# A transformer block's sum kernel: two attention-times-V blocks of a chunk joined, the last one moved within W2, and the next chunk's normalisation in other units

## The chip, the core and the metric

The kernel runs on one core of one Trainium2 chip. The metric is the device time of one execution in microseconds; the lower the better. Engines are named as the profile names them: PE is TensorE (matmuls), PEld its weight loads, DVE is VectorE, ACT is ScalarE, POOL is GpSimd, SP is SyncE, which issues most DMAs. ACTq and SPq are the DMA issues on ScalarE's and SyncE's own instruction queues.

## What is computed

All tensors are bf16: x is 1 x 2048 x 576, with 32 heads of 18, a causal window of 256 keys, and a gated feed-forward layer of width 4608. Both branches read the same normalised x, and the result is their sum with x.

```python
def _A_ref(x, wqkv, wo):
    B, S, D = x.shape
    H = 32; Dh = D // H; W = 256
    qkv = ...(x @ wqkv).reshape(B, S, 3, H, Dh)...
    scores = jnp.einsum("bhqd,bhkd->bhqk", q, k) * (Dh ** -0.5)
    mask = (idx[:, None] - idx[None, :] >= 0) & (idx[:, None] - idx[None, :] < W)
    p = _softmax(jnp.where(mask[None, None], scores, -1e9), axis=-1)
    o = jnp.einsum("bhqk,bhkd->bhqd", p, v)
    return ...(o)... @ wo

def _B_ref(x, w1, w3, w2):
    return (silu(x @ w1) * (x @ w3)) @ w2

xn = _layernorm(x, axis=-1)
return x + _A_ref(xn, A_wqkv, A_wo) + _B_ref(xn, B_w1, B_w3, B_w2)
```

## The kernel before

The 2048 rows go in four chunks of 512 (chunk 0 to 3, `c`). A chunk has three stretches on PE. First the projections of q, k and v (`PROJ`, line 490). Then 36 units of gate/up (`unit_pairs`, line 726): unit `u` makes 128 of the 4608 hidden columns in nine pairs of matmuls, one matmul of a pair on the upper and one on the lower 64 rows of the array, 512 columns each. Its two banks go through ACT (`unit_tanh`, line 735) and two DVE operations (`unit_h`, lines 741 and 744) into `hT[u]`; the second of these frees the unit's banks. Last W2 and the output projection (`p2_list`, `p2_item`, line 797), a list of steps of two matmuls each, counted by `n`.

Attention is spread between the units. Eight groups of four heads (`g`) have four score steps each in chunk 0 and five in the later chunks. A score step (`score_step`) is four or six matmuls of line 610 into the fixed banks 6 and 7 (`SC`), one exponential on ACT over both (line 619), and masks on POOL (line 646). The next score step overwrites those two banks, so it waits for that exponential. The exponentials stay in slots: `pt` (10), the stage tiles (4, `sh`), and the last tiles of `hT`, as long as their units have not come (`early`). `spaced_step` sets the steps by `clock`, a count of matmul pairs.

Two groups with all their steps done make one attention-times-V block (`pv`, line 667): 72 small matmuls in chunk 0 and 96 later, eight tiles of 64 x 32 of the array at once, into a pair of banks. There are four blocks (`j`) to a chunk. Blocks 0 to 2 stand behind a unit's last pair once `PV_AFTER` = 20 counts have passed, block 3 stands in W2 at step 8. A block is drained by two DVE transposes (`pv_out`, line 676), a reciprocal and a POOL multiplication for each half (`o_scale`, lines 681 and 682), two DVE transposes a half (`o_turn`, line 689), and DMAs into `oT` (`o_pack`, line 714): four, and for block 0 eight more small ones, which chunk 0 issues on ACT's queue, one a unit.

Banks 0 to 5 are three pairs (`JOBS`) that `job()` deals out in turn to projections, units and blocks alike; whoever gets a pair waits until its last reader is done. `add` records every operation with what it reads and writes; each engine executes its operations in the recorded order, and waits are worked out from the records. `later(u, ...)` puts work behind `unit_h` of unit `u`.

The next chunk's x tiles are normalised meanwhile: `loads` (SP), `stat` (three DVE operations and two on POOL), `apply` (two on DVE) and `xt` (`xn_send`, a DMA transpose on SP into the other half of `xnT`) name the units, in `near`: 20 to 40. Weights of a group of four units come in six DMAs on SP (`load_part`), two a unit, each behind a matmul.

## Time and profile before

| what | value |
|---|---|
| time, median of 3 runs | 558.03 us (557.90 to 558.07) |
| profiled execution: span from first to last instruction | 556.1 us |
| mean granted TensorE clock | 1.000 |
| attention-times-V matmuls (line 667) | 1440 in 16 blocks |
| gate/up matmuls (line 726), 64x512 | 2592 |
| W2 and wo matmuls (line 797), 64x288 | 2524, and 45 on all rows at the end |
| oT DMAs (line 714) issued on ACT's queue | 8, of 8 KB |

The profiled execution's own time is the span; the difference to the median lies before the first and after the last instruction. A row of the timeline gives the start and the length in microseconds of one instruction or of several like ones in a row (x4), then engine, line, operation, what it writes and reads, and in brackets how long the engine had been idle and what released it. The recorded length of a matmul has the depth of the pipeline in it, so two matmuls in a row overlap; from start to start is the pace.

### The profile page before, as it was taken

What the parts mean: (1) busy time and instruction counts of PE and PEld (TensorE: products, weight loads), DVE (VectorE), ACT (ScalarE), POOL (GpSimd) and SP (SyncE); (2) the same over time, 40 slices, a digit from 0 to 9 for tenths busy, and PEclk for the clock granted to TensorE, in tenths of its full rate; (3) what the DMA queues carried; (4) which work ended last, traced back from release to release, by engine and by line L of the source; (5) the groups of instructions that cost most, each with busy time, mean ns of one, the idle gap of its engine ahead of it and who ended that gap; (6) DMA issues with size and microseconds to landing.
All of it is one profiled execution on the core that took longest, in us unless ns stands there. A gap on an engine that the chain in (4) does not pass through costs nothing.

```text
span 556.1 us, 18239 instructions
## 1 busy us (share of the span) xinstructions
PE 552.4 (99%) x8022; PEld 348.8 (63%) x8022; DVE 310.8 (56%) x587; ACT 257.6 (46%) x365; POOL 160.0 (29%) x380
## 2 busy tenths in 40 slices
PE   8999999999999999999999999999999999999998
PEld 4555445677687455477767645547777654555776
DVE  7466798610456778851056668884105567767211
ACT  7456776100286767600047776650005676666000
POOL 5323454300034445330003344533000333433000
PEclk9999999999999999999999999999999999999999
DMA  9997899677566556656856746566683684650650
GB/s 255 203 197 161 201 215 182 171 179 191 139 139 149 135 147 151 155 148 176 205 109 137 171 110 170 126 163 164 158 205 83 138 174 124 151 135 21 174 152 22
DMA packets 128038, 86.00 MB, mean 155 GB/s; under 512 B 35702, under 2 KB 125646, under 8 KB 127958
## 3 DMA queue, kind: packets, MB, share of 16 engines
q1 hardware_dynamic: 89138, 62.80, 49.7%
q10 hardware_dynamic: 38820, 22.02, 16.0%
q8 instruction: 63, 1.03, 0.8%
q14 instruction: 17, 0.14, 0.1%
HBM read 71.29 MB, written 2.36 MB: 132 GB/s over the span
## 4 chain that ended last, share of the span: by engine, by line
PE 98%; DMA 1%; ACT 0%; DVE 0%; issue 0%
PE ps L726 51%; PE ps L797 29%; PE ps L490 10%; PE ps L610 6%; PE ps L667 4%; DMA xp<-in_A_x_dram 1%; DVE stats L386 0%; ACT hT L380 0%; PE ps L419 0%; ACT sd L359 0%; ACT xnT L432 0%; DVE ofin L819 0%; DVE mv L389 0%
## 5 line engine op out<-in xcount | busy, mean ns | idle before, releaser
L726 PE MATMUL ps<-xnT,w 64*128 64x512 bf16 x1400 | 182.3, 376 | 0.0
L726 PE MATMUL ps<-xnS,w 64*128 64x512 bf16 x1120 | 155.3, 376 | 0.0
L797 PE MATMUL ps<-w,hT 64*128 64x288 bf16 x2292 | 143.9, 282 | 0.0
L741 DVE SCALAR_TENSOR_TENSOR gs<-th,ps 128x512 bf16<-128x512 bf16 x144 | 98.0, 681 | 80.1 <-ACT th L735 79.1
L619 ACT ACTIVATE pt<-ps 128x1024 bf16<-128x1024 f32 (+1 forms) x112 | 113.2, 1010 | 63.8 <-PE ps L610 62.5
L797 PEld LDWEIGHTS ps<-w,hT 64*128 64x128 bf16 x2292 | 112.0, 94 | 29.4 <-issue 0.4
L726 PEld LDWEIGHTS ps<-xnT,w 64*128 64x128 bf16 x1400 | 73.8, 94 | 55.0
L646 POOL TENSOR_TENSOR pt<-pt,mk 128x128 int32<-128x128 int32 (+1 forms) x199 | 80.3, 426 | 79.5 <-ACT pt L619 79.5
L744 DVE SCALAR_TENSOR_TENSOR hT<-gs,ps 128x512 bf16<-128x512 bf16 x144 | 98.9, 687 | 5.0
L735 ACT ACTIVATE th<-ps 128x512 bf16<-128x512 f32 x144 | 85.4, 593 | 22.2 <-PE ps L726 21.9
L726 PEld LDWEIGHTS ps<-xnS,w 64*128 64x128 bf16 x1120 | 60.1, 94 | 50.1
L503 ACT ACTIVATE stage<-ps 128x512 bf16<-128x512 f32 x16 | 9.6, 597 | 142.8 <-PE ps L490 140.5
L828 DVE TENSOR_TENSOR ofin<-ps,xp 128x288 bf16<-128x288 f32 x31 | 12.2, 451 | 110.3 <-PE ps L797 110.3
L646 POOL TENSOR_TENSOR hT<-hT,mk 128x128 int32<-128x128 int32 (+1 forms) x31 | 12.4, 420 | 170.5 <-ACT hT L619 170.5
L610 PE MATMUL ps<-qv,kv 64*128 64x320 bf16 (+4 forms) x528 | 53.8, 260 | 0.0
L610 PEld LDWEIGHTS ps<-qv,kv 64*128 64x128 bf16 x528 | 28.5, 94 | 24.7 <-issue 0.3
L490 PE MATMUL ps<-xnT,wp 64*128 64x512 bf16 (+1 forms) x360 | 39.0, 355 | 0.0
L619 ACT ACTIVATE stage<-ps 128x1024 bf16<-128x1024 f32 x24 | 24.6, 1024 | 12.6 <-PE ps L610 12.6
L689 DVE STREAM_TRANSPOSE od<-oq 128x256 bf16<-128x256 bf16 x64 | 25.8, 428 | 6.3 <-POOL oq L682 6.3
L490 PEld LDWEIGHTS ps<-xnT,wp 64*128 64x128 bf16 x360 | 20.6, 94 | 12.6 <-ACT va L539 0.4
L490 PE MATMUL ps<-wv,xnT 64*128 64x288 bf16 x288 | 22.1, 284 | 0.2 <-ACT xnT L432 0.2
L646 POOL TENSOR_TENSOR stage<-stage,mk 128x128 int32<-128x128 int32 (+1 forms) x42 | 16.9, 421 | 17.4 <-ACT stage L619 17.3
(73 smaller groups left out, 337.6 us busy)
## 6 DMA issues: line engine op xcount, KB each, us to landing
w<-in_B_w_dram SPq DMA_DIRECT2D x210, 192.0 KB, 4.3
w<-in_B_w_dram ACTq DMA_DIRECT2D x70, 288.0 KB, 3.5
xp<-in_A_x_dram SPq DMA_DIRECT2D x29, 144.0 KB, 3.3
out_dram<-ofin SPq DMA_DIRECT2D x31, 72.0 KB, 3.2
xnS<-xnT SPq DMA_DIRECT2D x8, 256.0 KB, 5.2
oT<-od SPq DMA_DIRECT2D x56, 36.0 KB
pt<-in_A_wqkv_dram SPq DMA_DIRECT2D x4, 288.0 KB, 5.0
hT<-in_B_w_dram SPq DMA_DIRECT2D x6, 192.0 KB, 6.3
```

What stands on the lines that cost most here:

```text
L490: op = add("pe", lambda e, out_=out_, st=st, mv=mv, n=n, r0=r0, first=first: e.matmul(out_, st, mv, start=first, stop=(part == 1 and n == ...
L610: add("pe", lambda e, r0=r0, out_=out_, kb=kb, q0=q0, nb=nb: e.matmul(out_, kb4[r0:r0 + 64, g, kb + NV - NB, :] if kb < 0 else kv[r0:r0 + ...
L619: add("act", lambda e: e.activation(pt_slot(sl)[:, 0:w, :], PS[:, SC[0]:SC[1] + 1, 0:w].rearrange("p r q -> p q r"), ACT.Exp, scale=scale) ...
L646: add("pool", lambda e, vb=vb, mm=mm: e.tensor_tensor(vb, vb, mm, ALU.mult), r=(key if n == 0 else []) + ["mk"], **{"w" if n == 0 else "j" ...
L667: add("pe", lambda e, p=p, q=q, pr=pr, sl=sl, g=g, pos=pos, q0=q0, nb=nb, col=col, first=first, n=n: e.matmul(PS[32 * q:32 * q + VW, banks ...
L689: add("dve", lambda e: e.transpose(od[i][:, g % 2, c0:c0 + CH // 2], oq[:, c0:c0 + CH // 2]), r=["oq", "oq0"], **{"j" if half or g % 2 els ...
L726: op = add("pe", lambda e, n=n, r0=r0, r=r, k=k, src=src: e.matmul(PS[:, b0 + r, :], wt[r0:r0 + 64, k, fl * 128:(fl + 1) * 128], src, star ...
L735: add("act", lambda e: e.activation(th[i][:], PS[:, bg, :], ACT.Tanh, scale=0.5), r=[("ps", bg)], w=[("th", i)])
L741: add("dve", lambda e: e.scalar_tensor_tensor(out=gs[i][:], in0=th[i][:], scalar=1.0, in1=PS[:, bg, :], op0=ALU.add, op1=ALU.mult), r=[("t ...
L744: add("dve", lambda e: e.scalar_tensor_tensor(out=hT[:, u, :], in0=gs[i][:], scalar=0.5, in1=PS[:, bu, :], op0=ALU.mult, op1=ALU.mult), r= ...
L797: op = add("pe", lambda e: e.matmul(PS[:, bank, 0:w], stat, move, start=new, stop=False, skip_group_check=True, **tile), r=keys, after=hel ...
L828: add("dve", lambda e: e.tensor_tensor(ofin[:, o, :], PS[:, bank, 0:HD], xp[xs[n]][:, d0:d0 + HD], ALU.add), r=[("ps", bank), ("xp", xs[n] ...
```

## The change

Blocks 0 and 1 of a chunk become one (`BLOCKS`): two bank pairs are taken at once, and the matmuls of both stand together. The joined block's place is given by unit and pair (`AT`): before pair 0 of unit 21 in chunk 0, before pairs 4, 6 and 8 of unit 18 in chunks 1, 2 and 3. Its drain is recorded right there: four transposes, four reciprocals (each half has its own `rden` now), and the first multiplication; the halves 2 and 3 are held in two `pt` slots lent for it (`borrow`). Block 2 stands at least 36 counts after its last step. Chunks 1 to 3 start with eight slots in `hT` (`NHP`, tiles 20 to 35) instead of four, and chunk 0 may use the stage tiles too. Block 3 stands at step 58 of W2 instead of 8. The next x is loaded in units 2 and 5 and normalised in units 3 to 15; in chunk 0, whose loads stay, the first two tiles in units 14 to 19 and the others as before. Of block 0's eight small packs, two are issued a unit instead of one in chunk 0, still on ACT's queue.

```diff
@@ -202,6 +202,7 @@
 
         NXP, NOF, NPT, NW13, NW2, NOD, AHEAD = 7, 4, 10, 3, 4, 2, 6
         KB, NB, NV = 64, CH // 64, 12
+        NHP = 8
         ident = sb("ident", [128, 128])
         xp = [sb(f"xp{i}", [128, D]) for i in range(NXP)]
         xn = [sb(f"xn{i}", [128, 640]) for i in range(2)]
@@ -237,22 +238,23 @@
             if kind == "sh":
                 two = stage[:, 2 * n:2 * n + 2, :]
             else:
-                two = hT[:, NF - 8 + 2 * n:NF - 6 + 2 * n, :]
+                two = hT[:, NF - 2 * NHP + 2 * n:NF - 2 * NHP + 2 + 2 * n, :]
             return two.rearrange("p t c -> p (t c)").rearrange("p (q r) -> p q r", r=2)
 
         def pt_keys(sl):
             kind, n = sl
             if kind == "pt":
-                return [("pt", n)]
+                return [(kind, n)]
             if kind == "sh":
                 return [("sh", 2 * n), ("sh", 2 * n + 1)]
-            return [("h", NF - 8 + 2 * n), ("h", NF - 7 + 2 * n)]
+            t = NF - 2 * NHP + 2 * n
+            return [("h", t), ("h", t + 1)]
 
         def st_keys(*tiles):
             return [("sh", t) for t in tiles]
 
         uq = sb("uq", [128, CH], dt.float32)
-        rden = sb("rden", [128, CH // 32], dt.float32)
+        rden = [sb(f"rden{i}", [128, CH // 32], dt.float32) for i in range(4)]
         oq = sb("oq", [128, CH])
         od = [sb(f"od{i}", [128, 2, CH]) for i in range(NOD)]
         oT = sb("oT", [128, 5, CH])
@@ -672,16 +674,26 @@
                                     r=pt_keys(sl) + [("va", pos)], **{"j" if any(k[0] == p for k in seen - {(p, gi, pr)}) or not first else "w": [("ps", banks[p])]})
                     col += nb
 
+        def borrow(slots):
+
+            for i, n in enumerate(slots):
+                uqs[2 + i:3 + i] = [pt[:, n, :, :].rearrange("p q r -> p (q r)").bitcast(dt.float32)]
+                uq_keys[2 + i:3 + i] = [[("pt", n)]]
+
         def pv_out(b, i):
-            add("dve", lambda e: e.transpose(uqs[i], PS[:, b, :]), r=[("ps", b)], w=uq_keys[i])
+            to = uqs[i]
+            add("dve", lambda e: e.transpose(to, PS[:, b, :]), r=[("ps", b)], w=uq_keys[i])
+
+        def o_recip(i):
+            u3 = uqs[i].rearrange("p (n d) -> p n d", d=32)
+            add("dve", lambda e: e.reciprocal(rden[i][:], u3[:, :, Dh]), r=uq_keys[i], w=[("rden", i)])
 
         def o_scale(i):
             u3 = uqs[i].rearrange("p (n d) -> p n d", d=32)
             o3 = oq[:, :].rearrange("p (n d) -> p n d", d=32)[:, :, 0:Dh]
-            add("dve", lambda e: e.reciprocal(rden[:], u3[:, :, Dh]), r=uq_keys[i], w=["rden"])
             add("pool", lambda e: e.tensor_tensor(
-                o3, u3[:, :, 0:Dh], rden[:].unsqueeze(2).to_broadcast([128, CH // 32, Dh]), ALU.mult),
-                r=uq_keys[i] + ["rden", "oq0"], w=["oq"])
+                o3, u3[:, :, 0:Dh], rden[i][:].unsqueeze(2).to_broadcast([128, CH // 32, Dh]), ALU.mult),
+                r=uq_keys[i] + [("rden", i), "oq0"], w=["oq"])
 
         def o_turn(g, half):
             i = g // 2 % NOD
@@ -988,7 +1000,10 @@
 
         add("act", lambda e: e.preload_act_table_set("exp_and_others"))
 
-        PV_COST, PV_AFTER = 6.6, 20
+        PV_COST, BLOCKS = 6.6, ((0, 1), (2,))
+        PV_AFTER = (18, 18, 18, 18)
+        START = (60, 46, 46, 46)
+        AT = ((21, 0), (18, 4), (18, 6), (18, 8))
         main, rest = span_main, span_last
         late_spans = {0: [(main, 2, 5, 0, 1, "act")], 1: [(main, 2, 5, 1, 2, "act"), (main, 2, 5, 2, 5, "sp")],
                       **{u: [(rest, 2, 5, u - 2, u - 1, "act")] for u in (2, 3, 4)},
@@ -998,28 +1013,30 @@
         for c in range(NC):
             NS = len(steps_of(c))
             att = [(g, s) for g in range(G) for s in range(NS)]
-            near = {0: (20, 22, 23), 1: (24, 26, 27), 2: (30, 32, 33), 3: (33, 35, 40)}
+            near = {0: (3, 5, 6), 1: (6, 8, 9), 2: (9, 11, 12), 3: (12, 14, 15)}
+            if c == 0:
+                near = {0: (14, 16, 17), 1: (16, 18, 19), 2: (30, 32, 33), 3: (33, 35, 40)}
             plan = near if c + 1 < NC else {}
             stat, apply, xt = ({v[k]: i for i, v in plan.items()} for k in range(3))
-            loads = {8: (2,), 17: (3,)} if c + 1 < NC else {}
+            loads = {2: (2,), 5: (3,)} if c + 1 < NC else {}
             if c == 0:
                 loads = {11: (0,), 13: (1,), 15: (2,), 17: (3,)}
             total = 9 * NF + len(att) + 3 * PV_COST
             if c:
                 total += 9 * sum(COST[kind] for kind, _ in PROJ)
-            start = 60 if c == 0 else 46
+            start = START[c]
             last = total - 12
             nxt = soon = start
             clock = 0.0
             done = 0
             pv_ready = {}
             free = [("pt", n) for n in range(NPT)]
-            if c:
-                free += [("sh", n) for n in range(4)]
-            early = [("h", n) for n in range(4)]
+            free += [("sh", n) for n in range(4)]
+            early = [("h", n) for n in range(4 if c == 0 else 0, NHP)]
             side = {}
             jobs = {}
             next_pv = 0
+            turned = {}
 
             def later(u, what):
                 side.setdefault(u, []).append(what)
@@ -1033,20 +1050,61 @@
                 nonlocal done
                 g, s = att[done]
                 scores(c, g, s)
-                sl = take(done)
-                exps(c, g, s, sl)
+                exps(c, g, s, take(done))
                 masks(c, g, s)
                 done += 1
-                if done % (2 * NS) == 0:
-                    pv_ready[done // (2 * NS) - 1] = clock + PV_AFTER
+                for i, pairs in enumerate(BLOCKS):
+                    if done == 2 * NS * (pairs[-1] + 1):
+                        pv_ready[i] = clock + (36 if i else PV_AFTER[c])
 
             def spaced_step():
                 nonlocal nxt, soon, clock
                 score_step()
                 soon = clock + 7.5
-                room = last - clock - PV_COST * (3 - next_pv) - 5 * sum(v > at_u for v in xt)
+                room = last - clock - PV_COST * sum(map(len, BLOCKS[next_pv:])) - 5 * sum(v > at_u for v in xt)
                 nxt = max(soon, clock + room / max(1, len(att) - done))
                 clock += 1
+
+            def pv_block(u, mid=False):
+                nonlocal next_pv, clock, free, job_ctr, nxt, soon
+                block = BLOCKS[next_pv]
+                assert u > turned.get(c, -1) + 1, (c, u, turned)
+                next_pv += 1
+                pairs = [job() for _ in block]
+                for j, banks in zip(block, pairs):
+                    pv(c, j, banks)
+                clock += PV_COST * len(block)
+                if len(block) == 2:
+                    nxt, soon = max(nxt, clock + 9), max(soon, clock + 9)
+                groups = range(2 * block[0], 2 * block[-1] + 2)
+                was = [pt_of[(c, g, s)] for g in groups for s in range(NS)]
+                assert all(NF - 2 * NHP + 2 * n > u for kind, n in was if kind == "h"), (c, u)
+                was = [sl for sl in was if sl[0] != "h"]
+                lent = [n for kind, n in was if kind == "pt"][-2:] if len(block) == 2 else []
+                free += [sl for sl in was if sl not in [("pt", n) for n in lent]] + [("pt", n) for n in lent]
+
+                def drain(pairs=pairs, lent=lent):
+                    borrow(lent)
+                    for i in range(2 * len(pairs)):
+                        pv_out(pairs[i // 2][i % 2], i)
+                    for i in range(2 * len(pairs)):
+                        o_recip(i)
+                    o_scale(0)
+
+                drain() if mid else later(u, drain)
+                job_ctr += mid
+                k = 0
+                for i, g in enumerate(groups):
+                    for half in range(2):
+                        k += 1 if (i, half) not in ((0, 1), (2, 1)) else 0
+                        later(u + k, lambda g=g, half=half: o_turn(g, half))
+                    if i + 1 < len(groups):
+                        later(u + k, lambda i=i: o_scale(i + 1))
+                turned[c] = u + k
+                for i, j in enumerate(block):
+                    later(u + 4 + 3 * i, lambda j=j: o_pack(j, "sp"))
+                    for n in range(4, 12, 2) if j == 0 else ():
+                        later(u + n // 2 + 2 + (c > 0), lambda n=n: o_pack(0, "sp" if c else "act", n, n + 2))
 
             at_u = -1
             if c:
@@ -1076,8 +1134,10 @@
                 b0 = jobs[u] = job()
                 for n in range(9):
                     into = nxt - (clock + 9 - n)
-                    if done < len(att) and (clock >= nxt or (n == 8 and into < 3 and clock >= soon)):
+                    if done < len(att) and (done < len(early) or free) and (clock >= nxt or (n == 8 and into < 3 and clock >= soon)):
                         spaced_step()
+                    if next_pv == 0 and AT[c] == (u, n):
+                        pv_block(u, True)
                     op = unit_pairs(c, u, n, n + 1, b0[0])
                     clock += 1
                     if n in (3, 8):
@@ -1085,25 +1145,8 @@
                 unit_tanh(u, b0[0])
                 if u % 4 == 3 and u < NF - 8 and (c or u != 15):
                     owed += 6
-                if next_pv in pv_ready and clock >= pv_ready[next_pv] and next_pv < 3:
-                    j = next_pv
-                    next_pv += 1
-                    banks = job()
-                    pv(c, j, banks)
-                    clock += PV_COST
-                    for g in (2 * j, 2 * j + 1):
-                        for s in range(NS):
-                            if pt_of[(c, g, s)][0] != "h":
-                                free.append(pt_of[(c, g, s)])
-                    later(u, lambda b=banks: (pv_out(b[0], 0), pv_out(b[1], 1), o_scale(0)))
-                    later(u + 1, lambda j=j: (o_turn(2 * j, 0), o_turn(2 * j, 1), o_scale(1)))
-                    later(u + 2, lambda j=j: o_turn(2 * j + 1, 0))
-                    later(u + 3, lambda j=j: o_turn(2 * j + 1, 1))
-                    later(u + 5, lambda j=j: o_pack(j, "sp"))
-                    if j == 0:
-                        for n in range(4, 12, 1 if c == 0 else 2):
-                            later(u + n + 1 if c == 0 else u + n // 2 + 4,
-                                  lambda n=n: o_pack(0, "act", n, n + 1) if c == 0 else o_pack(0, "sp", n, n + 2))
+                if next_pv in pv_ready and clock >= pv_ready[next_pv] and (next_pv or not AT[c][1]):
+                    pv_block(u)
                 unit_h(u, b0[0])
                 for what in side.pop(u, []):
                     what()
@@ -1137,7 +1180,7 @@
                     load_w2(0, (u - 20) // 2, "act" if u < 24 else "sp")
                 if u == 31:
                     xs = [load_x(c * TB + tt) for tt in range(TB)]
-            assert done == len(att) and next_pv == 3, (done, next_pv)
+            assert done == len(att) and next_pv == len(BLOCKS), (done, next_pv)
             ACC[:] = [[*JOBS[job_ctr % 3], *SC], [*jobs[NF - 2], *jobs[NF - 1]]]
             assert len({*ACC[0], *ACC[1]}) == 8
             summed.clear()
@@ -1158,18 +1201,18 @@
                             what()
                 elif n == 8:
                     load_w2(c, AHEAD - 1, after=(last_pe(),))
+                elif n == 58:
                     banks = jobs[NF - 2]
                     pv(c, 3, banks)
-                    pv_out(banks[0], 0)
-                    pv_out(banks[1], 1)
-                    o_scale(0)
-                    o_turn(6, 0)
-                    o_turn(6, 1)
-                    o_scale(1)
-                    o_turn(7, 0)
-                    o_turn(7, 1)
+                    for i in range(2):
+                        pv_out(banks[i], i)
+                        o_recip(i)
+                    for i in range(2):
+                        o_scale(i)
+                        o_turn(6 + i, 0)
+                        o_turn(6 + i, 1)
                     o_pack(3, "sp")
-                elif n == 40 and c + 1 < NC:
+                elif n == 40 and c == 0:
                     xn_send((c + 1) * TB + 3)
                 elif n == 300 and c + 1 < NC:
                     xn_swap(c + 1, ("sp", "sp"))
```

2 lines of the change are left out of this document (1 added, 1 removed).

## The prediction, as it was made before the run

> **What bounds the kernel now.** I read the page first: the busy table, then the chain that ended last.
>
> ```profile
> span 556.1 us, 18239 instructions
> PE 552.4 (99%) x8022; PEld 348.8 (63%) x8022; DVE 310.8 (56%) x587; ACT 257.6 (46%) x365; POOL 160.0 (29%) x380
> ...
> PE 98%; DMA 1%; ACT 0%; DVE 0%; issue 0%
> ```
>
> TensorE is both 99% busy and 98% of the chain, so a change moves the end only by what it adds to or takes out of TensorE's queue. The span is 556.1 us and the median 558.03, so 1.9 us lie around the span; I make the sum against 556.1 and add it unchanged to 558.03. Next I read the order of both kernels' TensorE instructions: the same matmuls, only moved. What can change is the bubbles between shapes, and new waits. So I read the timeline around an attention-times-V block (chunk 0, unit 14; columns: start, duration, engine, line, operation, tiles, shapes, count):
>
> ```profile
> 51.92 0.40 PE L726 MATMUL ps<-xnT,hT 64*128 64x512 bf16 x2
> 52.25 0.32 PE L667 MATMUL ps<-hT,va 64*20 64x320 bf16 x4
> ...
> 53.07 0.23 PE L667 MATMUL ps<-pt,va 64*20 64x128 bf16 x4
> 53.23 0.37 PE L610 MATMUL ps<-qv,kv 64*128 64x320 bf16 x4
> ...
> 53.64 0.92 ACT L619 ACTIVATE pt<-ps 128x896 bf16<-128x896 f32 x1 [0.63 <-PE ps L610]
> ```
>
> and around the end of unit 13 of the same chunk, whose score step stands after six of its nine pairs:
>
> ```profile
> 49.11 0.40 PE L610 MATMUL ps<-qv,kv 64*128 64x320 bf16 x4
> 49.33 0.61 PE L726 MATMUL ps<-xnS,hT 64*128 64x512 bf16 x4
> 49.55 1.02 ACT L619 ACTIVATE pt<-ps 128x1024 bf16<-128x1024 f32 x1 [0.54 <-PE ps L610]
> 49.76 1.26 PE L726 MATMUL ps<-xnT,hT 64*128 64x512 bf16 x10
> 50.47 0.59 ACT L735 ACTIVATE th<-ps 128x512 bf16<-128x512 f32 x1
> 50.84 0.40 PE L726 MATMUL ps<-xnS,hT 64*128 64x512 bf16 x2
> 51.09 0.69 DVE L741 SCALAR_TENSOR_TENSOR gs<-th,ps 128x512 bf16<-128x512 bf16 x1 [0.64 <-ACT th L735]
> 51.81 0.69 DVE L744 SCALAR_TENSOR_TENSOR hT<-gs,ps 128x512 bf16<-128x512 bf16 x1
> ```
>
> Five pairs take 50.84 - 49.76 = 1.08 us, so a pair takes 0.216 and streams without a gap. A score step of 512 columns takes one pair's time (49.11 to 49.33). Durations on the rows hold the pipeline's depth; starts count.
>
> **Part 1, the join: -0.8 us.** Into the block: 52.25 - 51.92 = 0.33, less the pair's 0.216, leaves 0.11. Out: 53.23 - 53.07 = 0.16, less 128 columns (a quarter pair, 0.054), leaves 0.11; the groups' starts are staggered by some 0.02, so I take 0.10 each. Joining two blocks drops one entry and one exit, 0.2 us a chunk, 0.8 in four. Bounds: 0.15 to 0.22 a chunk. The last block in W2 keeps both its bubbles.
>
> **Part 2, the wait that the join brings to chunk 0: +1.6 us.** A joined block takes two bank pairs at once. There are three pairs and the unit in progress holds one, so the second half of the block needs the pair of the unit just finished. In the built order chunk 0's block stands between the last pair of unit 20 and the first of unit 21, and the first matmul of its second half waits for VectorE's second operation (hT) of unit 20. Unit 20 has its score step after six pairs, as unit 13 above: its streaming ends at T (49.76 + 0.216 = 49.98 there), the exponential holds ScalarE until 50.57, tanh starts at 50.47, and hT ends at 51.81 + 0.69 = 52.50, T + 2.5. The first half of the block starts at T + 0.1 and takes 0.9 (52.25 to 53.23 less the exit), so the second is due at T + 1.0 and waits 1.5, and about 0.05 more for the semaphore (tanh ends at 51.06, gs starts at 51.09). TensorE is in order: units 21 and on stand behind it. Bounds: 1.3, if tanh weren't held by the exponential (chunk 1's unit 14 below, hT at T + 2.25), to 1.75, if an entry is paid again.
>
> **Part 3, the same wait in chunks 1 to 3: 0.** There the block stands inside unit 18, after 4, 6 and 8 pairs and one score step. Unit 17 of chunks 1 and 2 has its score step after three pairs, as unit 14 of chunk 1 here:
>
> ```profile
> 188.00 0.38 PE L610 MATMUL ps<-qv,kv 64*128 64x320 bf16 x6
> ...
> 189.29 0.81 PE L726 MATMUL ps<-xnT,w 64*128 64x512 bf16 x6
> 189.72 0.60 ACT L735 ACTIVATE th<-ps 128x512 bf16<-128x512 f32 x1 [0.27 <-PE ps L726]
> ...
> 191.07 0.69 DVE L744 SCALAR_TENSOR_TENSOR hT<-gs,ps 128x512 bf16<-128x512 bf16 x1
> ```
>
> It ends at 189.29 + 0.216 = 189.51; tanh starts 0.2 and hT ends 2.25 later. In chunk 1 the second half is due 4 x 0.216 + 0.216 + 0.1 + 1.2 = 2.38 after the end of unit 17 (1.2: chunk 1's half has 2560 columns to chunk 0's 1920, 0.9 x 4/3). That leaves 0.07 beyond the semaphore; chunk 2 has 0.43 more. In chunk 3 unit 17's score step follows eight pairs, hT comes some 2.9 after the end (exponential from T to T + 1.02, tanh 0.6, two operations 1.4), and the half is due at 3.24. Upper bound 0.1 a chunk. The banks go on to units 19 and 20; VectorE's four transposes (0.64 apart, rows in part 5) free the first pair before unit 19 in chunks 1 and 2, and within 0.05 us of it in chunk 3.
>
> **Part 4, two DMA issues a unit on ScalarE's queue in chunk 0: +1.2 us.** The eight small oT packs went one a unit; now two follow the tanh of each of units 25 to 28. What two issues do shows in chunk 0's unit 21, where a pack and a W2 load meet:
>
> ```profile
> 66.53 0.60 ACT L735 ACTIVATE th<-ps 128x512 bf16<-128x512 f32 x1 [0.27 <-PE ps L726]
> 66.53 0.64 ACTq L714 DMA_DIRECT2D oT<-od  x1
> 66.75 0.38 PE L610 MATMUL ps<-qv,kv 64*128 64x320 bf16 x6
> 66.97 0.59 PE L726 MATMUL ps<-xnT,w 64*128 64x512 bf16 x4
> 67.21 0.87 ACTq L352 DMA_DIRECT2D w<-in_B_w_dram  x1
> 68.13 1.02 ACT L619 ACTIVATE pt<-ps 128x1024 bf16<-128x1024 f32 x1 [1.01 <-PE ps L726]
> ...
> 68.69 0.61 ACTq L714 DMA_DIRECT2D oT<-od  x1
> ```
>
> The scores were ready at 66.97, an exponential starts 0.22 later (49.33, 49.55), but this one began at 68.13, 0.05 after the second issue ended. So issues block ScalarE. Two packs take 0.64 + 0.04 + 0.61 = 1.3 from 0.2 after a unit's end T: the next exponential starts at T + 1.55. Its successor in the order, the next score step, overwrites the same two banks and waits for it. Units 25 to 29 have their steps after 5, 4, 3, 2 pairs, then between 28 and 29 and after 7:
> - Unit 25's first issue also waits for the turn (0.43) behind unit 24's hT (T24 + 2.5), that is until T25 + 0.75. The exponential of unit 26 (0.92) then runs from T25 + 2.1 to 3.0; unit 27's step is due at T25 + 2.13 + 0.65 = 2.78: 0.3 late with the semaphore.
> - Unit 28's exponential (1.02) runs from T27 + 1.55 to 2.57; the step behind unit 28 is due at T27 + 2.16: 0.45 late.
> - The step after that is due 2.16 after its predecessor's due time plus the 0.45 already lost, against 2.57 from T28: 0.45 again.
>
> Bounds: 0 if issues ran beside the exponential after all, 1.6 with the first issue's 0.71 instead of 0.61 and a later turn. I take 1.2, the row's own spacing. The Trainium skill (DMA: Bandwidth & Descriptors, Issuing engines are not separate DMA queues) says that the sequencer's time to start a DMA is usually small beside the transfer; by it this term would be 0 and the sum that of the first rival.
>
> **Part 5, the fourth block 50 steps later in W2: 0.** Chunk 1's W2:
>
> ```profile
> 240.49 16.71 PE L797 MATMUL ps<-w,hT 64*128 64x288 bf16 x270
> 240.73 0.70 DVE L676 STREAM_TRANSPOSE uq<-ps 128x512 f32<-128x512 f32 x1
> 241.37 0.67 DVE L676 STREAM_TRANSPOSE ofin<-ps 128x512 f32<-128x512 f32 x1
> ...
> 244.65 0.77 DVE L689 STREAM_TRANSPOSE od<-oq 128x256 bf16<-128x256 bf16 x2 [0.79 <-POOL oq L682]
> 245.45 3.00 SPq L714 DMA_DIRECT2D oT<-od  x4
> ...
> 257.03 2.12 PE L797 MATMUL ps<-wo,oT 64*128 64x288 bf16 x32
> ```
>
> A step is two matmuls of 16.71/270 = 0.062, so 50 are 6.2 us. The drain's packs are issued by 248.45; the first matmul that needs them is 16 behind 257.03, at 258.0. That is 9.5 us of cover less 6.2 = 3.3 for landing; like transfers land in 3.2 (out) to 4.3 (w):
>
> ```profile
> w<-in_B_w_dram SPq DMA_DIRECT2D x210, 192.0 KB, 4.3
> ...
> out_dram<-ofin SPq DMA_DIRECT2D x31, 72.0 KB, 3.2
> ```
>
> Landing counts from issue, and the last issue starts 0.75 before 248.45, which gives 4.0. The reciprocals, now ahead, take a further 0.7 off the drain, as the first scaling runs beside the second transpose. I take 0; if the cover failed, 0.3 a chunk. On SP nothing of W2 stands before the pack but, in chunk 0, one xn transpose that no longer stands behind it.
>
> **Part 6, next x normalised in units 3 to 15 (chunks 1, 2; 14 to 19 for chunk 0's first two): 0.** Units 0 to 5 of chunk 1:
>
> ```profile
> core 0: us, PE busy (x) PEld busy (x) DVE busy (x) ACT busy (x) POOL busy (x), PEclk, DMA share, GB/s
> 155.12:168.31 13.19, 13.19 (x149) 11.56 (x145) 8.01 (x13) 10.22 (x14) 4.86 (x13) 1.00 0.69 146
> ```
> ```profile
> L386 DVE BATCH_NORM_STATS2 stats<-xp 128x6 f32<-128x288 bf16 x30 | 12.1, 442 | 0.3 <-DMA xp<-in_A_x_dram 0.3
> ...
> L681 DVE RECIPROCAL rden<-uq 128x16 f32<-128x16 f32 x16 | 3.4, 211 | 0.0
> ```
>
> VectorE has 5.2 of 13.2 us free, 0.85 a unit, and one tile's statistics (two of 0.44) take about that; a unit's banks come round only three units on. The x loads and xn transposes go to SP as before, only earlier, and the oT packs of chunks 1 to 3 later. There the xn transpose waits for the scaling, and weight loads queue behind it, each for a buffer used two weight blocks (eight units, 17 us) later. If that cover went, a unit would wait the 1 us of the hold. The more and other exponential slots change no instruction's length.
>
> **Sum:** -0.8 + 1.6 + 1.2 = +2.0: span 558.1, time 560.0 us.
>
> **Rivals.**
> - *Issues cost nothing* (20%): part 4 falls to 0, from the point where an issue ends before the exponential is due. Against: the row at 68.13. For: no single pack delayed TensorE before. 558.03 - 0.8 + 1.6 = 558.8.
> - *Not slower* (5%): chunk 0's second half finds its banks free and the packs fit too. Place: between units 20 and 21; it decides if hT of unit 20 ends within 1.0 us of the unit. Against: it ended 2.25 to 2.5 after in both rows. 558.03 - 0.8 = 557.2.
> - *The drain holds banks in every chunk* (12%): four transposes and four reciprocals stand before the unit's own two operations, 4 x 0.64 + 4 x 0.21 = 3.4 us of VectorE; if unit 19 or 21 of chunks 1 to 3 waits 0.4 for it, +1.2: 561.2. Against: the arithmetic of part 3 leaves all but chunk 3 clear.
> - The change not doing what it says: chunk 0's block isn't inside a unit at all; that is part 2.
>
> **How the numbers follow.** 63% for 560.0. Its own range is 559.2 to 560.9 (1.3 to 1.75, 0.8 to 1.6, 0.6 to 0.9). Taking in issues at 0 below and the drain above gives 558.5 to 561.2. About 0.2%, 1.1 us, is what can be told from no change: slower needs 559.15, which the forecast and the third rival clear for the most part, 72%; the second and first rival and the forecast's low end lie within, 25%; faster, under 556.9, would need gains that no row shows, 3%.
>
> **What would show it.** Right: in the changed profile one gap of some 1.6 us on TensorE inside chunk 0's joined block ended by VectorE's hT, none in chunks 1 to 3; score steps near units 27 to 29 of chunk 0 waiting 0.3 to 0.5 for ScalarE; four fewer 0.2 us bubble pairs; W2 without a gap before wo. Wrong: exponentials that start during issues, waits at units 19 to 21 or at wo, or a chunk 0 as long as before.

## The result and the profile after

The changed kernel takes 564.62 us (median of 4 runs, 563.06 to 565.13) against 558.01 us before (557.90 to 558.07; 558.03 was the median of the three runs known ahead): 1.0113 times, with an interval of 1.0099 to 1.0127. The forecast was 560.0 us in 558.5 to 561.2; the loss is 6.6 us where 2.0 were expected. The profiled execution took 564.81 us and spans 563.1 us, 7.0 more than before.

The page of the changed kernel (busy table, queue table, chain of waits):

```profile
span 563.1 us, 18248 instructions
...
PE 553.0 (98%) x8022; PEld 377.2 (67%) x8022; DVE 312.8 (56%) x587; ACT 260.0 (46%) x365; POOL 160.5 (29%) x380
...
q8 instruction: 63, 1.03, 0.8%
...
PE 94%; DMA 2%; DVE 2%; ACT 1%; issue 1%; ACTq 1%; SPq 0%
```

TensorE does the same 8022 matmuls in nearly the same busy time (552.4 us before); its share of the chain fell from 98% to 94%, and DMA, VectorE, ScalarE, its queue and "issue" have the rest. So TensorE stands still in a few places. To find them I took, for each unit, the time from its first matmul to the first of the next unit and subtracted the streaming of the columns in between (a pair 0.213 us, other shapes by their columns). A wait ahead of a unit's first matmul counts to the unit before it. A unit without a gap shows 0.02 to 0.05 by this measure; a single attention-times-V block adds some 0.3 for its bubbles in chunk 0 and 0.35 to 0.45 in the others. What is left, in us, by chunk and unit:

| place | before | after | what ended the gap after |
|---|---|---|---|
| chunk 0, unit 17 | 0.03 | 3.00 | VectorE's hT, late |
| chunk 0, unit 19 | 0.03 | 0.22 | the same |
| chunk 0, joined block (units 14 and 21 before, 20 after) | 0.66 | 2.00 | hT of units 19 and 20 |
| chunk 0, unit 22 | 0.03 | 1.42 | "issue": nothing on a semaphore |
| chunk 0, units 27, 28, 29 (without a block) | 0.09 | 1.35 | ScalarE's exponential |
| chunk 0, all | 1.84 | 9.05 | |
| chunk 1, units 18 and 19 (joined block and behind it; before, its two blocks stood in units 8 and 17 with 0.87) | 0.06 | 0.88 | bubbles 0.58; 0.27 "issue" |
| chunk 1, all | 2.18 | 2.20 | |
| chunk 2, all | 2.12 | 2.10 | 0.22 "issue" in unit 20 |
| chunk 3, all | 2.10 | 1.98 | |

Chunk 0 lost 7.2 us, the rest gained 0.1. The rows of the changed kernel's timeline behind it (start, duration, engine, line, operation, tiles, shapes, count, and in brackets the idle time and what ended it; lines have moved: unit matmuls are L738, scores L612, attention times V L669, exponential L621, statistics L388, oT packs L726):

```profile
54.57 0.60 SPq L298 DMA_DIRECT2D xp<-in_A_x_dram  x1
...
59.05 0.82 DVE L388 BATCH_NORM_STATS2 stats<-xp 128x6 f32<-128x288 bf16 x2 [4.70 <-DMA xp<-in_A_x_dram]
...
60.70 0.69 DVE L756 SCALAR_TENSOR_TENSOR hT<-gs,ps 128x512 bf16<-128x512 bf16 x1
...
61.44 0.39 PE L738 MATMUL ps<-xnT,w 64*128 64x512 bf16 x2 [2.79 <-DVE hT L756]
...
69.56 0.32 PE L669 MATMUL ps<-hT,va 64*20 64x320 bf16 x4 [1.09 <-DVE hT L756]
...
70.88 0.77 PE L669 MATMUL ps<-pt,va 64*20 64x320 bf16 x44 [0.27 <-DVE hT L756]
...
75.76 0.35 PE L612 MATMUL ps<-qv,kv 64*128 64x320 bf16 x3
77.33 0.23 PE L612 MATMUL ps<-qv,kv 64*128 64x128 bf16 x1 [1.22 <-issue]
...
84.80 1.38 ACTq L726 DMA_DIRECT2D oT<-od  x2
...
86.22 0.92 ACT L621 ACTIVATE pt<-ps 128x896 bf16<-128x896 f32 x1 [1.30 <-DVE gs L753]
...
87.20 0.37 PE L612 MATMUL ps<-qv,kv 64*128 64x320 bf16 x4 [0.18 <-ACT pt L621]
...
91.29 0.39 PE L612 MATMUL ps<-qv,kv 64*128 64x320 bf16 x6 [0.27 <-ACT pt L621]
...
93.43 0.36 PE L612 MATMUL ps<-qv,kv 64*128 64x320 bf16 x4 [0.24 <-ACT pt L621]
```

Four stories, read from the top. (1) The x tile that VectorE is to take statistics of behind unit 14 (which ends at 52.0) is loaded by an instruction that the program has at unit 11 (43.2 us), but SP, behind with weight loads and key copies, issues it only at 54.57, and it lands at 59.0. VectorE stands 4.70 us in front of it with the hT operations of units 15 to 17 queued behind, the banks don't come free, and TensorE waits 2.79 between units 17 and 18. (2) The joined block waits at its entry for hT of unit 19 and inside for that of unit 20. (3) In unit 22 TensorE pauses between the third and fourth matmul of one score step, for nothing that a semaphore explains. (4) The pairs of oT packs hold ScalarE's queue (the row at 84.80 is one of them), an exponential starts late, and the score step after it waits: three times.

### The profile page after: what moved, and what is told of

Read it like the earlier page. It is cut to its first block, busy times and chain, and to the rows that moved or that the text cites. A ratio compares the mean times of both kernels' runs of the same rounds, so it can differ in the third digit from the quotient of the medians.

```text
span 563.1 us, 18248 instructions
## 1 busy us (share of the span) xinstructions
PE 553.0 (98%) x8022; PEld 377.2 (67%) x8022; DVE 312.8 (56%) x587; ACT 260.0 (46%) x365; POOL 160.5 (29%) x380
## 3 DMA queue, kind: packets, MB, share of 16 engines
q10 hardware_dynamic: 38820, 22.02, 15.6%
q8 instruction: 63, 1.03, 0.8%
HBM read 71.29 MB, written 2.36 MB: 131 GB/s over the span
## 4 chain that ended last, share of the span: by engine, by line
PE 94%; DMA 2%; DVE 2%; ACT 1%; issue 1%; ACTq 1%; SPq 0%
PE ps L738 48%; PE ps L809 28%; PE ps L492 10%; PE ps L612 5%; PE ps L669 3%; DMA xp<-in_A_x_dram 2%; ACTq L726 1%; DVE hT L756 0%; DVE gs L753 0%; ACT pt L621 0%; DVE stats L388 0%; DVE xn L406 0%; ACT th L747 0%; SPq L322 0%; ACT hT L382 0%
## 5 line engine op out<-in xcount | busy, mean ns | idle before, releaser
L738 PE MATMUL ps<-xnT,w 64*128 64x512 bf16 x1400 | 190.0, 376 | 3.0 <-DVE hT L756 2.8
L738 PE MATMUL ps<-xnS,w 64*128 64x512 bf16 x1120 | 159.3, 376 | 0.0
L738 PEld LDWEIGHTS ps<-xnT,w 64*128 64x128 bf16 x1400 | 89.0, 94 | 50.1 <-DVE hT L756 3.3
L621 ACT ACTIVATE pt<-ps 128x1024 bf16<-128x1024 f32 (+1 forms) x92 | 93.3, 1014 | 44.7 <-PE ps L612 42.3
L738 PEld LDWEIGHTS ps<-xnS,w 64*128 64x128 bf16 x1120 | 69.8, 94 | 37.4
L648 POOL TENSOR_TENSOR pt<-pt,mk 128x128 int32<-128x128 int32 (+1 forms) x165 | 67.9, 433 | 56.5 <-ACT pt L621 56.5
L648 POOL TENSOR_TENSOR hT<-hT,mk 128x128 int32<-128x128 int32 (+1 forms) x52 | 20.7, 420 | 165.3 <-ACT hT L621 165.3
L612 PE MATMUL ps<-qv,kv 64*128 64x320 bf16 (+4 forms) x528 | 57.4, 260 | 1.9 <-issue 1.2
L612 PEld LDWEIGHTS ps<-qv,kv 64*128 64x128 bf16 x528 | 33.6, 94 | 22.3 <-ACT pt L621 2.5
L621 ACT ACTIVATE stage<-ps 128x1024 bf16<-128x1024 f32 (+1 forms) x32 | 32.1, 1003 | 16.2 <-PE ps L612 16.2
L621 ACT ACTIVATE hT<-ps 128x1024 bf16<-128x1024 f32 (+1 forms) x28 | 28.4, 1015 | 10.0 <-PE ps L612 9.9
L648 POOL TENSOR_TENSOR stage<-stage,mk 128x128 int32<-128x128 int32 (+1 forms) x55 | 21.6, 412 | 27.4 <-ACT stage L621 27.1
```

Source lines behind the costliest of these rows:

```text
L612: add("pe", lambda e, r0=r0, out_=out_, kb=kb, q0=q0, nb=nb: e.matmul(out_, kb4[r0:r0 + 64, g, kb + NV - NB, :] if kb < 0 else kv[r0:r0 + ...
L621: add("act", lambda e: e.activation(pt_slot(sl)[:, 0:w, :], PS[:, SC[0]:SC[1] + 1, 0:w].rearrange("p r q -> p q r"), ACT.Exp, scale=scale) ...
L648: add("pool", lambda e, vb=vb, mm=mm: e.tensor_tensor(vb, vb, mm, ALU.mult), r=(key if n == 0 else []) + ["mk"], **{"w" if n == 0 else "j" ...
L738: op = add("pe", lambda e, n=n, r0=r0, r=r, k=k, src=src: e.matmul(PS[:, b0 + r, :], wt[r0:r0 + 64, k, fl * 128:(fl + 1) * 128], src, star ...
```

## The experiments

The third story had no cause yet, and the others were read from one execution, so each was tried. Theory A is the late load, theory B a lack of room on VectorE; theory D, that TensorE's instructions themselves come late behind a joined block, was formed after the first four runs. Diffs are against the changed kernel; where a run builds on another, the text says so, and "..." stands for lines left out.

**The load alone, and the statistics alone.**

```diff
-                loads = {11: (0,), 13: (1,), 15: (2,), 17: (3,)}
+                loads = {5: (0,), 7: (1,), 15: (2,), 17: (3,)}
```

> Only the two loads of the next chunk's first two x tiles move on SP's queue, from units 11 and 13 of chunk 0 to units 5 and 7; statistics and normalising stay in units 14 to 19, and TensorE's, VectorE's, ScalarE's and GpSimd's orders are those of the changed kernel. Theory A (late load: VectorE stood 4.70 us in front of the first statistics because the load landed at 59.05, hT of units 15 to 17 came late, TensorE waited 2.79 us in unit 17): the gap goes and the time falls by 3.2 us (3.0 in unit 17, 0.2 in unit 19), 564.6 to 561.4. Theory B (VectorE has no room for the statistics in units 14 to 19, whenever the data comes): 564.6 stays, or at most 1 us goes.

Measured: 561.78 us (561.11 to 562.34), 1.0067 of before (1.0055 to 1.0079), so 2.8 us come back by moving two DMA issues. The timeline of this run:

```profile
38.95 0.60 SPq L298 DMA_DIRECT2D xp<-in_A_x_dram  x1
...
54.33 0.81 DVE L388 BATCH_NORM_STATS2 stats<-xp 128x6 f32<-128x288 bf16 x2
...
67.77 0.77 PE L669 MATMUL ps<-pt,va 64*20 64x320 bf16 x44 [0.87 <-DVE hT L756]
```

Issued 15.6 us earlier, the load has landed (at 46.1) when VectorE comes to it: no wait in front of the statistics, and unit 17 shows 0.03 over its streaming where it had 3.00. VectorE does the statistics in units 14 to 19, and none of these units shows a gap. A holds, B falls. That the time came within 0.4 of the forecast is in part luck: unit 22's gap shrank from 1.42 to 0.27 by itself, and the "issue" gaps of chunks 1 and 2 grew by 0.79 and 0.38. The wait inside the joined block grew from 0.27 to 0.87 as the one at its entry shrank: whichever hT was late before, the block ends 0.9 us after hT of unit 20, and its excess stays at 2.0.

```diff
-                near = {0: (14, 16, 17), 1: (16, 18, 19), 2: (30, 32, 33), 3: (33, 35, 40)}
+                near = {0: (20, 22, 23), 1: (24, 26, 27), 2: (30, 32, 33), 3: (33, 35, 40)}
...
-                room = last - clock - PV_COST * sum(map(len, BLOCKS[next_pv:])) - 5 * sum(v > at_u for v in xt)
+                room = last - clock - PV_COST * sum(map(len, BLOCKS[next_pv:])) - 5 * sum(v > at_u for v in (xt if c else (17, 19, 33, 40)))
```

> Statistics, transposes and normalising of chunk 0's first two next tiles go back to the units of the kernel before (20, 22, 23 and 24, 26, 27), the loads stay; TensorE's order is that of the changed kernel. Theories A and B alike: the wait of 2.79 us in unit 17 goes, 561.4. They differ only with the run above: A gives both runs the same time within 0.4 us, B has this one 2 us or more faster. A third reading (the normalising work now falls into the drain of the joined block in units 21 to 24): 562 to 563 here.

Measured: 563.58 us (562.64 to 563.75). The gap in unit 17 is gone here too, as is the one in unit 22 (0.03), but unit 27 has 1.12 (0.43 with the change), chunk 1's unit 19 has 1.42 and chunk 2's unit 20 0.90. The first fits the third reading, that statistics, drain and packs now meet in units 21 to 27; its number (562 to 563) was too low. The other two are "issue" gaps in chunks in which nothing was edited, and they are larger than in the changed kernel. So A's forecast of the same time for both runs, within 0.4, failed by 1.8: other terms moved too. B, by which this run was to be the faster one, fails all the same.

**The packs.**

```diff
-                        later(u + n // 2 + 2 + (c > 0), lambda n=n: o_pack(0, "sp" if c else "act", n, n + 2))
+                        later(u + n // 2 + 2 + (c > 0), lambda n=n: o_pack(0, "sp", n, n + 2))
```

> The eight small oT packs of chunk 0 are issued from SP's queue and not from ScalarE's, all else as in the changed kernel. Theory (issues block ScalarE, the 0.40, 0.45 and 0.41 us that units 27, 28 and 29 of chunk 0 show over their streaming): 564.6 - 1.26 = 563.3, and the exponentials of units 26 to 28 wait for no issue. Rival (the issues lie beside other work, the three gaps come from VectorE's drain or from the score schedule): 564.6, gaps unchanged. A second rival: eight more issues on SP delay W2's first weight blocks: over 564.6.

Measured: 564.64 us (562.53 to 565.24), no change in the median. By that alone the rival would stand. The profile says otherwise: units 27, 28 and 29 show 0.03, 0.03 and 0.08 where they had 0.43, 0.48 and 0.44, which is 1.2 us saved as expected; chunk 1's unit 19 and chunk 2's unit 20 give 1.25 of it back. In the profiled execution (565.24) unit 22 has no gap either, another 1.4 saved, but that is lost to one more thing, which shows in this view by windows (busy time of the engines in each window, then the granted clock of TensorE):

```profile
core 0: us, PE busy (x) PEld busy (x) DVE busy (x) ACT busy (x) POOL busy (x), PEclk, DMA share, GB/s
58.00:60.00 2.00, 0.73 (x8) 0.17 (x3) 1.03 (x4) 0.28 (x1) 0.00 (x0) 1.00 1.12 243
60.00:62.00 2.00, 0.67 (x6) 0.31 (x8) 1.93 (x4) 0.60 (x1) 1.83 (x5) 0.85 1.04 222
62.00:63.00 1.00, 1.00 (x12) 0.45 (x10) 0.81 (x2) 0.65 (x1) 0.07 (x1) 0.50 0.53 161
63.00:64.00 1.00, 1.00 (x8) 0.41 (x6) 0.97 (x4) 0.38 (x1) 0.07 (x1) 0.50 0.73 233
64.00:65.00 1.00, 1.00 (x10) 0.33 (x6) 0.97 (x4) 0.00 (x0) 0.92 (x3) 0.58 0.99 227
```

After the wait in unit 17 (2.60 us here) the clock is granted at 0.50 for 3.41 us by the trace's clock records, and unit 18 takes 1.7 us longer. In the profile of the changed kernel a wait of 2.79 at the same place was followed by a clock of 1.00. So a wait of this length has a second price, in some executions only. The Trainium skill (TensorE: Matmul & The Clock Gate, What's actually happening) has the clock halved after an idle window of about 3.4 us that runs freely. The 3.41 us agree with the length of that window, but that it must be idle from end to end is not borne out: TensorE was busy for 0.81 of the 3.41 us before the halving. Why the wait of 2.79 left the clock alone is not shown.

**The bank wait of chunk 0's joined block.**

```diff
-        AT = ((21, 0), (18, 4), (18, 6), (18, 8))
+        AT = ((21, 8), (18, 4), (18, 6), (18, 8))
```

> Chunk 0's joined block moves from ahead of unit 21's first pair to ahead of its last (eight pairs and one score step later); the rest of the orders follows. Theory (second half waits for hT of unit 20, forecast 1.6 us, in the profile 2.0 above the streaming of the block): the block starts after hT of unit 20 has ended, no wait inside it, 564.6 - 1.6 = 563.0. Rival (what costs time is what the block's 144 matmuls and 144 weight loads leave behind: 1.2 us without any wait in unit 22): the wait goes and the gap behind the block stays, so 563.0 with the gap of over 1 us moved along, or 564.6 if the drain, one unit later against units 22 and 23, takes it back.

Measured: 565.71 us (563.45 to 568.30), 1.0142 of before (1.0118 to 1.0165), so no faster. The wait inside the block is gone, as the theory has it: the block's unit shows 0.39 in place of 2.00. But behind it (timeline of this run):

```profile
73.06 0.51 PE L612 MATMUL ps<-qv,kv 64*128 64x320 bf16 x3
76.30 0.23 PE L612 MATMUL ps<-qv,kv 64*128 64x128 bf16 x1 [2.74 <-issue]
```

Unit 22 grew from 1.42 over its streaming to 3.30, and unit 23 has 1.71, with the clock granted at 0.50 from 77 to 80 us. The rival named in the expectation is right on the place, the gap behind the block, but both its numbers were too low: the gap did not only stay but grew. As I read it, the bank wait had been hiding part of another wait.

What is that other wait? I counted the instructions of TensorE's queue from the start of the program: matmuls, weight loads and the 87 semaphore and drain instructions that the trace has between them. The gap of unit 22 stands at instruction 1729 in both kernels, to within one; those of chunks 1 and 2 stand at 5569 and 9665 in every run so far. These lie 15 and 16 times 256 apart. (Without the semaphore instructions the count misses: the gaps come at about 1713, 5531 and 9607.) The queue table above shows 63 transfers of kind "instruction" with 1.03 MB, 16 KB each, for 2 x 8022 + 87 = 16131 instructions: one for every 256. In the trace the transfers nearest to these gaps run from 74.29 to 75.64 (gap ends 77.33) in the changed kernel and from 73.34 to 74.66 (gap ends 76.30) here. The Trainium skill (Runtime: NRT & Kernel Launch, Instruction fetch mechanics) says that each engine's instructions are refilled in blocks of 16 KB, 256 instructions, while it executes, and that the cost is mostly hidden. The size agrees with the counts here; that it is hidden doesn't. A joined block uses 288 matmuls and loads (chunk 0) or 384 in about 2 us; a plain unit uses some 45 in 2.1. This became theory D.

**Three runs for theory D.** The first is the base of the others: both edits of the x loads and of the packs.

> Both edits together: the two x loads at units 5 and 7, and chunk 0's eight small packs on SP's queue. If the two savings stand side by side: 561.8 - 1.26 = 560.5. Rival (TensorE's 'issue' gaps in units 19 to 22 of the chunks grow by what the others shrink, since what TensorE waits for there comes at a time of its own): 561.8 again, with the gaps of units 27 to 29 of chunk 0 gone and those behind the joined blocks of chunks 1 and 2 at 0.5 to 1.4 us.

Measured: 561.13 us (559.96 to 564.13), between the two. Units 27 to 29 show 0.03, 0.05 and 0.11, but the units with instructions 1729, 5569 and 9665 have 0.66, 1.33 and 1.27 over their streaming. The one of chunk 1 in the timeline:

```profile
202.22 1.03 PE L738 MATMUL ps<-xnS,w 64*128 64x512 bf16 x8
204.39 1.25 PE L738 MATMUL ps<-xnT,w 64*128 64x512 bf16 x10 [1.14 <-issue]
```

It stands between two pairs of a plain unit, after the block has ended: no block, bank or semaphore is in play there. The next diff comes on top of these two edits:

```diff
-        PV_COST, BLOCKS = 6.6, ((0, 1), (2,))
+        PV_COST, BLOCKS = 6.6, ((0,), (1,), (2,))
-        AT = ((21, 0), (18, 4), (18, 6), (18, 8))
+        AT = ((99, 0),) * 4
...
-                        pv_ready[i] = clock + (36 if i else PV_AFTER[c])
+                        pv_ready[i] = clock + 20
...
-                if next_pv in pv_ready and clock >= pv_ready[next_pv] and (next_pv or not AT[c][1]):
+                if next_pv in pv_ready and clock >= pv_ready[next_pv] and u > turned.get(c, -1) + 1 and (next_pv or not AT[c][1]):
```

> As the run above, but the first two blocks of each chunk stand by themselves again, at the units where the kernel before has them; early normalising, score slots and the fourth block in W2 stay as changed. Theory D (a joined block takes 288 to 384 TensorE instructions off the queue in about 2 us, and the next 256 are not there in time: gaps at TensorE instructions 1729, 5569 and 9665, multiples of 256 apart): the gaps behind the blocks go, chunk 0 loses its bank wait too. Against the run above: chunk 0 -1.7, chunk 1 -0.9, chunk 2 -0.35, chunk 3 +0.25, so 560.5 - 2.7 = 557.8. Rival (those gaps come from the drain or the score slots, which stay): only chunk 0's bank wait goes and the bubbles come back, -1.4 + 0.6: 559.7.

Measured: 560.78 us (559.66 to 563.77). Every "issue" gap is gone, and chunks 1, 2 and 3 stand at 2.23, 2.25 and 2.15 in sum, as before the change; that part is as D has it. The time isn't 557.8, and by itself it is no nearer to D than to its rival (559.7). The timeline shows the reason:

```profile
76.52 1.31 SPq L726 DMA_DIRECT2D oT<-od  x2
77.88 1.33 SPq L322 DMA_DIRECT2D w<-in_B_w_dram  x2
79.25 1.30 SPq L726 DMA_DIRECT2D oT<-od  x2
80.60 2.63 SPq L322 DMA_DIRECT2D w<-in_B_w_dram  x4
...
84.99 0.82 PE L738 MATMUL ps<-xnT,w 64*128 64x512 bf16 x6 [2.17 <-DMA w<-in_B_w_dram]
```

The small packs, on SP now and seven units earlier than with the join, are threaded among the loads of a gate/up weight block, and unit 27 waits for the block: 2.36 us. It is like the second rival of the run with the packs on SP, at a place where it bites.

The next diff, too, comes on top of the first run's two edits:

```diff
-        warm(4, [CH] * 9)
+        warm(4, [CH] * 6)
+        for k in range(64):
+            p, q = 0, k % 4
+            add("pe", lambda e, p=p, q=q: e.matmul(
+                PS[32 * q:32 * q + VW, 4, 32 * (k // 4):32 * (k // 4) + 32], oq[64 * p:64 * p + 64, 0:VW], oq[64 * p:64 * p + 64, 0:32],
+                start=True, stop=True, tile_position=(64 * p, 32 * q), skip_group_check=True),
+                r=["oq0"], j=[("ps", 4)])
```

> As the first run of this call, with 64 tiny warm-up matmuls in place of three long ones in the first 5 us, which move every later TensorE instruction 122 places on in the instruction stream and change nothing else. The output is the same. Theory D: the steps of 256 now fall inside the joined blocks (chunk 1: block at places 5242 to 5625, steps at 5313 and 5569), a whole 256 is used up in some 1.5 us where the run without shift shows 4.7 to 5.8 us to bring the next: a gap of some 3 us inside the block of chunks 1 and 2, up to 3 in chunk 3, 1 to 2 in chunk 0; 564 to 570. Rival (the gaps are a matter of semaphores, banks or slots): the same time as the first run within 0.4 us, gaps at the same places of the program.

Measured: 570.13 us (567.26 to 573.89), 9.0 us more than the base, for 64 tiny matmuls in the first 5 us of the program. (The profiled executions are 5.9 apart. All six runs of this kernel had a granted clock of 0.991 to 0.997 on average, where the six of the base had 1.000, so the half clock is in the 9.0 too. In the profile it came at 69.50 us for 3.41 us, in a wait of 1.38 us behind one of 0.92.) The timeline of this run inside the joined blocks of chunks 1 and 3, and the total of TensorE's waits of this kind from the view of waits (us, times, longest):

```profile
201.75 0.25 PE L669 MATMUL ps<-pt,va 64*20 64x128 bf16 x3
204.33 0.21 PE L669 MATMUL ps<-pt,va 64*20 64x128 bf16 x1 [2.33 <-issue]
...
483.37 0.22 PE L669 MATMUL ps<-pt,va 64*20 64x128 bf16 x2 [1.84 <-issue]
```
```profile
PE ps L669 <- issue: 7.3, 4, 2.3
```

The gaps are now in the middle of the blocks, at instructions 5569, 9665 and 13761 again, though these are other matmuls than before: 122 places earlier in the program. Chunk 3, which had none, has one. The place in the instruction stream sets the gap, not the work that stands there, and a semaphore cannot explain that; D is shown. A size of mine was off: in chunks 1 to 3 the next 256 were there 3.5 to 4.2 us after the last boundary was crossed, not 4.7 to 5.8, so the gaps are 1.9 to 2.5 and not 3.

**What is left of the change without the four costs.** The join only in chunk 3, single blocks elsewhere, small packs one a unit on ScalarE's queue:

```diff
-        PV_COST, BLOCKS = 6.6, ((0, 1), (2,))
+        PV_COST = 6.6
...
+            BLOCKS = ((0, 1), (2,)) if c == 3 else ((0,), (1,), (2,))
...
-                    for n in range(4, 12, 2) if j == 0 else ():
-                        later(u + n // 2 + 2 + (c > 0), lambda n=n: o_pack(0, "sp" if c else "act", n, n + 2))
+                    for n in range(4, 12, 1 if c == 0 else 2) if j == 0 else ():
+                        later(u + (n // 2 + 3 if c else n + 1), lambda n=n: o_pack(0, "sp" if c else "act", n, n + (2 if c else 1)))
...
```

> The join only in chunk 3, where the profiles show no instruction gap; chunks 0 to 2 with single blocks at the units of the kernel before; x loads at units 5 and 7, small packs one a unit on ScalarE's queue as before; early normalising, score slots and the fourth block in W2 as changed. If the four found costs (late load, bank wait, issues, instruction supply) are all there is: chunks 0 to 2 as in the kernel before, chunk 3 0.2 us shorter: 557.8 against 558.0. If early normalising, slots or the block in W2 cost something by themselves: over 558.3. If W2's landings or the packs go late as in the not joined run, a wait of 2 us at a weight block shows in chunk 0: about 560.

Measured: 558.37 us (557.54 to 559.01), 1.0002 of before (0.9993 to 1.0011). Chunks 1 to 3 stand at 2.18, 2.19 and 1.94 where they were 2.18, 2.12 and 2.10. Chunk 0 keeps 0.6 at unit 21, by this run's timeline:

```profile
67.18 1.81 ACTq L354 DMA_DIRECT2D w<-in_B_w_dram  x1
69.04 1.02 ACT L621 ACTIVATE stage<-ps 128x1024 bf16<-128x1024 f32 x1 [1.95 <-PE ps L738]
```

A W2 load's issue on ScalarE's queue took 1.81 us (0.87 in the kernel before), and an exponential stood behind it. Why it took longer is open.

> As the join in chunk 3 alone, but chunk 0 has the x loads and the normalising at the units of the kernel before, so its TensorE order is that of the kernel before up to W2. If all that is left of the change (early normalising in chunks 1 and 2, slots, fourth block in W2, join in chunk 3) costs nothing and the join saves 0.2: 557.8 to 557.9 against 558.0, within 0.2% either way. If chunk 0 keeps 0.6 us over its streaming at unit 21 (a W2 load's issue of 1.81 us ahead of an exponential in the run before), that excess does not come from the normalising: 558.4.

This run also has chunk 0's x loads and normalising at the units of before. Measured: 557.77 us (557.58 to 558.15) against 558.01, 0.9993 (0.9984 to 1.0002). Its chunk 0 is at 1.88 (1.84 before), chunk 3 at 1.94 (2.10). The 0.6 us at unit 21 are gone, with 1.13 us for that issue; one execution of each kernel cannot tell whether the place of the normalising did it. It is the fastest of all, but by an amount that the measurement can't tell from nothing.

## Why the prediction was wrong

Its direction was right, and so were the two costs that it had, nearly; two more were missing, worth 5 of the 7 us. By its own parts, with the sizes of the profiled execution:

- *Part 1, the join, -0.8.* The bubbles go the way that was worked out, by less: chunk 3, which has nothing else, gained 0.07 to 0.17 in every run with the join but the shifted one, where 0.2 was forecast and 0.15 the lower bound. But the part priced a join by its bubbles alone. That 288 or 384 instructions in a row outrun the supply of instructions was nowhere among the parts or rivals: 1.4 us behind chunk 0's block, 0.27 and 0.22 in chunks 1 and 2, which ate the 0.2 that each of them gained. This is the first missing term, 1.9 us here, and as it depends on when a transfer lands, it is probably what spreads the changed kernel's runs over 2 us, where those before lie within 0.2.
- *Part 2, the wait in chunk 0's block, +1.6.* Right in releaser and size: the block's excess of 2.00 less the bubbles of one block, 0.3, is 1.7, and hT of unit 20 ended 2.55 us behind its unit, where 2.5 was forecast. The place was right in part: 1.09 of the wait stood at the block's entry, for hT of unit 19, which the forecast did not have (0.43 with the loads early). As the block ends by hT of unit 20 either way, this did not change the sum.
- *Part 3, no wait in chunks 1 to 3.* Right: the joined blocks there show their bubbles only, and the third rival (the drain holds banks everywhere) has nothing for it.
- *Part 4, two issues a unit on ScalarE, +1.2.* Right in all three places: 0.40, 0.45 and 0.41 against 0.3, 0.45 and 0.45. By the sentence of the Trainium skill beside it (DMA: Bandwidth & Descriptors, Issuing engines are not separate DMA queues) the term was to be 0, the first rival. An issue of 0.6 to 0.7 us is small beside the 3.1 to 7.1 us that the changed kernel's profile gives from issue to landing, but it costs time here, as another instruction of that queue is due within the 1.4 us that two issues take.
- *Part 5, the fourth block in W2, 0.* Right; W2 has no gap, and the last run keeps this part at no cost.
- *Part 6, next x normalised earlier, 0.* This is the step that failed. For chunks 1 and 2 it holds. For chunk 0's first two tiles it took VectorE's free time (0.85 us a unit) and the buffers behind the transposes as the cover, and said of the loads only that they go to SP as before. But the loads were not moved, the statistics were, by six units, and the cover of a read is the time from the landing of its data. SP ran some 11 us behind the program there (the load stands at unit 11, 43.2 us, and was issued at 54.57). The row for it was in the timeline of the kernel before too, and the prediction did not look at it:

```profile
54.27 0.60 SPq L296 DMA_DIRECT2D xp<-in_A_x_dram  x1
```

  With the statistics behind unit 20 that was early enough; behind unit 14 VectorE comes to them at 54.35 (59.05 - 4.70), the moment of the issue. With VectorE in order, 4.70 us of its wait became 2.97 of TensorE's in unit 17 and 0.2 more in unit 19.

Sum: 3.2 (part 6) + 1.4 (part 2 and the join in chunk 0, 2.00 + 0.03 - 0.66) + 1.3 (part 4) + 1.4 (instructions, chunk 0) - 0.1 (chunks 1 to 3, their instruction gaps among it) = 7.2 (7.1 before rounding), against 7.0 between the spans.

The first rival (558.8) fails with part 4 and the second (557.2) with part 2. Why the instructions come later behind some blocks than behind others is settled in part: chunk 3's joined block, cut by the boundaries at the same places, showed no such gap unless the stream was shifted. In the changed kernel the instruction transfers begin near the boundaries, one to each. After the boundary inside the joined block (1473, 5313, 9409 and 13505 in chunks 0 to 3) the transfer began 4.07, 2.23, 1.98 and 1.05 us later and took 1.2 to 1.4; the gaps of chunks 0 to 2 ended 1.2 to 1.7 us after it. The view by windows has the two microseconds behind each of these boundaries:

```profile
core 0: us, PE busy (x) PEld busy (x) DVE busy (x) ACT busy (x) POOL busy (x), PEclk, DMA share, GB/s
70.22:72.22 2.00, 1.73 (x108) 1.16 (x99) 2.00 (x4) 0.00 (x0) 0.00 (x0) 1.00 1.33 152
203.76:205.76 2.00, 2.00 (x118) 1.49 (x109) 1.71 (x3) 0.00 (x0) 0.62 (x2) 1.00 1.06 214
341.45:343.45 2.00, 2.00 (x121) 1.56 (x111) 1.67 (x3) 0.00 (x0) 0.20 (x1) 1.00 1.02 219
479.09:481.09 2.00, 2.00 (x120) 1.61 (x111) 1.69 (x3) 0.19 (x1) 0.65 (x2) 1.00 0.22 52
```

The DMA engines were full in the first three windows (a packet counts with its whole time where it starts, so the share can pass 1); in the fourth their share was 0.22. Chunk 3's transfer ended at 481.33, before TensorE came to the next boundary at 483.16. That the other traffic holds the transfer up fits these rows; no run changed that traffic alone, so it is not shown.

## What to carry to other kernels

When a read moves earlier, check the issue time of its load in the trace, not the load's place in the program: a queue that runs 11 us behind turns "off the critical path" into a wait of everything behind the reader. Bunching many small matmuls together saves the bubbles between shapes only as long as the engine's instructions keep coming; look for TensorE gaps that no semaphore ends, and for whether they stand at a fixed count of instructions. And when an edit that removes a gap doesn't move the time, look at the other gaps before dropping the reason: here they grew by what the edit had saved.

## What the runs showed of the hardware

- TensorE's instruction supply: 16 KB, or 256 instructions, a transfer (63 for 16131 instructions of its queue). Joined blocks left gaps of 0.2 to 3.3 us at instruction counts that lie multiples of 256 apart; 122 instructions more at the start of the program cost 9.0 us on 561.
- A wait of 2.6 to 2.8 us on TensorE was followed in two profiles, not in a third, by 3.41 us at a granted clock of 0.50, which cost 1.7 us; in another it came in a wait of 1.38 behind one of 0.92.
- The issue of chunk 0's first W2 load on ScalarE's queue took 0.39 to 0.43 us in eight profiles, 0.87 and 1.13 in two and 1.81 in one.
